# Packing two row groups for the last input transposes, and reading the parameter columns in one matmul, in a gated state-space and feed-forward kernel

## The chip, the cores and the metric

The kernel runs on one core of one Trainium2 chip. The metric is the device time of one execution in microseconds (us). The engines are named as in the profile: PE is TensorE (PEld its weight loads), DVE is VectorE, ACT is ScalarE, POOL is GpSimd, and SP is SyncE, which here only issues DMAs. ACT issues DMAs too; "SPq" and "ACTq" mark such issues. Row numbers such as L433 are lines of the kernel before the change.

## The reference

The input x has 2048 tokens of 448 values, in bf16. Three results are made of it and mixed token by token:

```python
g = sigmoid((x * gate_w).sum(-1, keepdims=True))
dt = exp(log_dt); Lam_bar = exp(dt * (Lambda_re + 1j * Lambda_im))
h[t] = Lam_bar * h[t-1] + B_bar @ x[t]          # complex scan over 2048 tokens, 448 states
a = 2 * real(C @ h[t]) + x * Dskip
b = silu(x @ w1) @ w2                           # 448 -> 1792 -> 448
out = g * a + (1 - g) * b
```

`B_bar` is B scaled by `(Lam_bar - 1) / Lam`. The three parameter vectors `log_dt`, `Lambda_re` and `Lambda_im` have 448 values each, one for each state.

## The kernel before

**Tiling.** The 2048 tokens are read as 1024 pairs: a row of `x2` is an even token followed by the odd one after it, 896 values. The feed-forward part works in four chunks of 512 tokens (even tokens first half and second half, then the odd ones). Its hidden width of 1792 is 14 blocks of 128 columns, taken two at a time. TensorE contracts over partitions, so x must be turned with features on partitions: three full groups of 128 features (j = 0, 1, 2) and a rest of 64 (j = 3, columns 384 to 447). A rest of 64 fills only half of the array's rows, so the kernel runs two matmuls side by side, one on partitions 0 to 63 ("LO") and one on 64 to 127 ("UP"). For that the rest of x has to lie on both halves: in `XT[0:64, 3, :]` and, copied, in `XR[64:128, :]`.

**The order of the work** is written out by hand. Each operation is given to an engine in program order, and a tracker (`Tracker`, L43 to L148) adds a semaphore wait for every read or written key that another engine or a DMA has touched. Each engine takes its list strictly in that order.

**The start.** Most of x is turned by DMA transposes, but the first chunk (tokens 0 to 511 of the even ones) is needed sooner. It is loaded as it lies, in four row groups k of 128 tokens (`XH[:, k, :]`, keys XA0 to XA3, and XB0 and XB1 for the later columns, which are the loads XA[4] and XA[5] in the code), and turned on TensorE by a matmul against the identity `ID`. `turn_k(j, k)` (L489) turns feature group j of row group k into PSUM; `turned_k` and `turned_x` (L499 to L508) are the DVE copies of the result into `XT`. Four such transposes per feature group are 16 in all, at L491. Between them TensorE begins the first six blocks of the hidden layer: `ffn1_first` (L427 to L441) is a generator that holds six PSUM banks open, contracts j = 0 over tokens 0 to 255 and then 256 to 511, and then j = 1 and j = 2 over all 512. Before anything has landed, `warm` (L477) runs 20 matmuls on ones, and two more ahead of the first real block (L515).

The rest (j = 3) is turned by four transposes at L535, each of 128 columns of which only the first 64 are used. `turned_x(3)` (L570) copies the 512 columns to `XT[:, 3, 0:512]`, and L571 copies the lower half of the same PSUM tile to `XR[64:128, 0:512]`. `ffn1_rem` (L443) then contracts the rest for two blocks at once, LO from `XT` and UP from `XR`, 512 columns each, three times for the six banks; after each, `ffn1_act` (L453) has ACT take Silu of two banks into `AT` (L455). From there on `pair` (L373) and `lanes` (L360, matmuls at L365) carry TensorE through the other blocks: a pair needs two free PSUM banks, and the first pair after the six banks that has to wait for one is the one that reuses the banks of `ffn1_act(0, 0)`.

**The parameters.** `log_dt`, `Lambda_re` and `Lambda_im` are loaded as three rows of `R` (`ld_row`, L261). DVE copies the last 64 values to a second place (`rd`, L465), four matmuls against four columns of `ID` turn the rows into four columns of 128 states each (`mm_cols`, L469), and one DVE copy brings them to `PV` (L528). ACT computes `dt` with Exp (L565), DVE makes the phase and `dt * Lambda_re` (L566 to L568), ACT makes `mag` with Exp (L569), and then loads the table with Silu by a small dummy activation (L572) before the first `ffn1_act`. A dummy Exp (L292) loads the Exp table early. The phase columns go on to POOL and DVE, which fill the rotation tables `FP`, `G` (L610 to L617).

**The queues.** Loads of x and of `w1` are issued on SP and ACT in turn (L275 to L301); ACT also issues the broadcasts of `gate_w` and `A_Dskip` (`GWB`, `DB`, L300 and L301), which DVE needs in `gate` and `skip` (L646 to L661). POOL makes `ID` and `IOTA` and clears a few columns (L324 to L332), and then waits for the phase columns.

Of the kernel before, what the change touches and what calls it, by code (L numbers as in the profile page):

```python
# [8 lines left out]
AF = mybir.ActivationFunctionType  # L9
# [141 lines left out]
def gated_mix(nc, A_x, A_Lambda_re, A_Lambda_im, A_B_re, A_B_im, A_C_re, A_C_im, A_log_dt,  # L151
              A_Dskip, B_x, B_w1, B_w2, gate_w, out):
    with ExitStack() as ctx:
# [3 lines left out]
        def sb(name, shape, dtype):  # L157
            return E(nc.sbuf_tensor(name, list(shape), dtype))
# [31 lines left out]
        R = sb("R", [128, 512], BF16)  # L190
        PV = sb("PV", [128, 4, 4], F32)
# [33 lines left out]
        def ld(eng, dst, src, key, group=None):  # L225
            return T.dma(eng, lambda e: e.dma_start(dst, src), writes=[key], group=group)  # L226
# [5 lines left out]
        XE = [(["XTe000", "XTe001", "XTe010", "XTe011", "XTe02"], ["XTe03"]), (["XTe1"], ["XTer1"])]  # L232
# [17 lines left out]
        def row(v):  # L250
            return v.rearrange("(o n) -> o n", o=1)
# [9 lines left out]
        def ld_row(eng, i, v):  # L261
            ld(eng, R[i:i + 1, 0:D], row(v), f"R{i}", gR if i < 2 else gR2)
# [23 lines left out]
        ld("sp", XH[:, 2:4, 384:512], x0[:, 2:4, 384:512], XA[5])  # L286
        gE = [ld_wr(eng, c, False) for c, eng in enumerate(("sp", "act"))]
# [4 lines left out]
        T.op("act", lambda e: e.activation(JK[:, 0:1], HP[:, :], AF.Exp), reads=["HP"], writes=["JK0"])  # L292
# [6 lines left out]

        ld_b(GWB, gate_w, "GW")  # L300
        ld_b(DB, A_Dskip, "DB")  # L301
# [29 lines left out]
        for pt in range(4):  # L331
            T.op("pool", lambda e, pt=pt: e.memset(HS[:, 2 * pt:2 * pt + 2, 0:8], 0.0), writes=[f"HSz{pt}"])  # L332
        SGN = ["SGa", "SGb"]
# [93 lines left out]
        def ffn1_first():  # L427
            banks = [nxt() for _ in range(NF1)]
            for j, h in ((0, 0), (0, 1), (1, None), (2, None)):
                c = slice(0, 512) if h is None else slice(256 * h, 256 * h + 256)  # L430
                for n, fb in enumerate((0, 2, 4, 1, 3, 5)):
                    bank = banks[fb]
                    T.op("pe", lambda pe, fb=fb, bank=bank, j=j, h=h, c=c: pe.matmul(  # L433
                        ps[:, bank, c], W1E[:, j, ff(fb) * 128:(ff(fb) + 1) * 128], XT[:, j, c],
                        start=(h == 0), stop=(h == 0), skip_group_check=(h != 0)),
                        reads=[f"W1Ej{j}" if j else f"W1Ej0{fb % 2}"] + (
                            ["XTe02"] if j == 2 else [f"XTe0{j}{h}"] if h is not None else [f"XTe0{j}0", f"XTe0{j}1"]),
                        writes=[f"ps{bank}"])
                    if (j, h, n) in ((0, 0, 3), (0, 0, 5), (1, None, 2), (1, None, 5)):
                        yield  # L440
            yield banks  # L441

        def ffn1_rem(banks, fb):  # L443
            def mm(pe):
                ins = None
                for i, p in enumerate((LO, UP)):
                    ins = pe.matmul(ps[:, banks[fb + i], :], w1(fb + i)(p, 3), xh(0, 0, 3, p), start=False, stop=True,  # L447
                                    skip_group_check=True)
                return ins
            T.op("pe", mm, reads=rem_ffn1(0, 0, fb), writes=[f"ps{banks[fb]}", f"ps{banks[fb + 1]}"])  # L450
            ffn1_act(0, fb, banks[fb], 2)
# [13 lines left out]
        def rd():  # L465
            T.op("dve", lambda e: e.tensor_copy(R[0:3, D:512], R[0:3, 384:448]), reads=["R0", "R1", "R2"],
                 writes=["Rd"])

        def mm_cols(pe):  # L469
            ins = None  # L470
            for pt in range(4):
                ins = pe.matmul(ps[:, 7, 256 + pt * 8:260 + pt * 8], R[:, pt * 128:(pt + 1) * 128],  # L472
                                ID[:, 0:4], start=True, stop=True)
            return ins
# [40 lines left out]
        warm(2, 4)  # L515
# [6 lines left out]
        for k in (2, 3):  # L522
# [5 lines left out]
        T.op("dve", lambda e: e.tensor_copy(  # L528
            PV[:, :, :], ps[:, 7, 256:288].rearrange("p (t c) -> p t c", c=8)[:, :, 0:4]),
            reads=["pv", "ps7"], writes=["PV"])  # L530
# [4 lines left out]
        for i in range(2):  # L535
            turn_x(3, i)
# [16 lines left out]
        LDT, LRE, LIM = PV[:, :, 0], PV[:, :, 1], PV[:, :, 2]  # L553
# [16 lines left out]
        turned_x(3)  # L570
        T.op("dve", lambda e: e.tensor_copy(XR[64:128, 0:512], xp[3][0:64, :]), reads=["ps7"], writes=["XR0a"])  # L571
        T.op("act", lambda e: e.activation(JK[:, 0:1], HP[:, :], AF.Silu), reads=["HP"], writes=["JK0"])  # L572
        pts("phr", col("phf"), MAGIC, -MAGIC, ALU.add, ALU.add, ["phf"])
# [688 lines left out]
```

## Time and profile before

| what | value |
|---|---|
| median of 3 runs | 136.72 us (136.67 to 136.77) |
| the profiled execution | 136.72 us, of which its span is 135.3 us |
| PE busy | 131.9 us, 97% of the span |
| DVE, ACT, POOL busy | 114.2, 93.7, 15.1 us |
| granted TensorE clock, all windows | 1.00 |
| DMA busy from 3 to 9 us | 0.96 to 0.98 of 16 engines |

The profile is of one execution. Times in it are microseconds from the start of the span; the 1.4 us between 135.3 and 136.72 lie outside the span. "Busy" counts instructions in flight, and TensorE's are pipelined, so the distance from one matmul's start to the next says more than its duration. A chain of waits leads from the last instruction back to what released it at each step; a timeline lists one engine's instructions in order, with start, duration, and in brackets the idle time before one and what ended it.

### The profile page before, as it was taken

How to read it: one execution, taken by the hardware profiler on the slowest of the kernel's cores; microseconds unless marked ns; L12 is line 12 of the kernel's file. 1: busy time of each engine (PE TensorE's matmuls, PEld its weight loads, DVE VectorE, ACT ScalarE, POOL GpSimd, SP SyncE). 2: the span in 40 equal slices, each digit the busy share in tenths (PEclk: the TensorE clock that was granted, in tenths of full speed). 3: DMA queues.
4: the chain of work that ended last, by engine and by line, in shares of the span. 5: the costliest groups of instructions: out<-in, count | busy, mean ns of one | idle time of the engine just before them, and what ended most of it. 6: DMA issues, size and time to landing. Idle time of an engine off the chain costs nothing.

```text
span 135.3 us, 2630 instructions
## 1 busy us (share of the span) xinstructions
PE 131.9 (97%) x1072; PEld 65.7 (49%) x1073; DVE 114.2 (84%) x152; ACT 93.7 (69%) x146; POOL 15.1 (11%) x32
## 2 busy tenths in 40 slices
PE   7899999999999999999999999999999999999993
PEld 7554444444444554444445544445555555555552
DVE  1467898917899798999999999999999999994554
ACT  0369888899939999768999597797113437879200
POOL 7108768050000000000000000000000000000000
DMA  4999979999897220000122000000000000222123
GB/s 109 273 278 162 157 153 244 181 286 300 251 184 123 55 62 0 0 0 0 44 56 60 5 0 0 0 5 0 0 0 0 0 0 7 100 89 81 68 78 126
DMA packets 24928, 11.95 MB, mean 88 GB/s; under 512 B 16851, under 2 KB 24406, under 8 KB 24918
## 3 DMA queue, kind: packets, MB, share of 16 engines
q1 hardware_dynamic: 22996, 10.43, 32.3%
q10 hardware_dynamic: 1922, 1.37, 3.6%
q8 instruction: 8, 0.13, 0.4%
q14 instruction: 2, 0.02, 0.0%
HBM read 5.51 MB, written 1.84 MB: 54 GB/s over the span
## 4 chain that ended last, share of the span: by engine, by line
PE 94%; DMA 3%; DVE 1%; ACTq 1%; issue 0%
PE ps L365 44%; PE ps L794 16%; PE ps L809 16%; PE ps L1047 15%; DMA XN<-in_A_x_dram 3%; PE ps L433 3%; DVE TMPS L1071 1%; ACTq L226 1%; PE ps L491 1%; PE ps L447 1%; PE ps L472 0%
## 5 line engine op out<-in xcount | busy, mean ns | idle before, releaser
L365 PE MATMUL ps<-XT,W1E 64*128 64x512 bf16 x325 | 41.3, 376 | 0.0
L455 ACT ACTIVATE AT<-ps 128x1024 bf16<-128x1024 f32 x28 | 28.2, 1019 | 7.4 <-PE ps L365 7.2
L365 PEld LDWEIGHTS ps<-XT,W1E 64*128 64x128 bf16 x325 | 16.9, 94 | 19.0 <-ACT AT L455 0.3
L365 PE MATMUL ps<-XT,BT 64*128 64x512 bf16 x156 | 22.4, 376 | 0.0
L809 PE MATMUL ps<-W,AT 64*128 64x448 bf16 x224 | 21.5, 349 | 0.0
L794 PE MATMUL ps<-W,AT 128*128 128x448 bf16 x112 | 21.4, 353 | 0.0
L794 PEld LDWEIGHTS ps<-W,AT 128*128 128x128 bf16 x112 | 10.9, 98 | 10.5 <-issue 0.4
L809 PEld LDWEIGHTS ps<-W,AT 64*128 64x128 bf16 x224 | 10.9, 94 | 10.4
L838 ACT ACTIVATE BT<-ps,GT 128x448 bf16<-128x448 f32 x8 | 5.1, 634 | 13.2 <-PE ps L794 13.2
L894 DVE SCALAR_TENSOR_TENSOR HS<-VE,P,ps 128x512 bf16<-128x512 bf16 (+1 forms) x13 | 9.6, 780 | 3.9 <-PE ps L365 3.9
L365 PEld LDWEIGHTS ps<-XT,BT 64*128 64x128 bf16 x156 | 8.1, 94 | 9.3 <-DVE HS L894 0.4
L938 DVE TENSOR_TENSOR_SCAN G<-P,Q 128x1024 f32<-128x1024 f32 (+1 forms) x6 | 11.4, 1923 | 0.0
L1047 PE MATMUL ps<-CO,VE 128*128 128x448 bf16 (+2 forms) x63 | 11.1, 332 | 0.0
L1047 PE MATMUL ps<-CO,HS 128*128 128x448 bf16 x56 | 11.1, 352 | 0.0
L365 PE MATMUL ps<-XR,W1E 64*128 64x512 bf16 x25 | 9.2, 376 | 0.0
L1047 PEld LDWEIGHTS ps<-CO,VE 128*128 128x128 bf16 x63 | 6.0, 98 | 4.8
L1047 PEld LDWEIGHTS ps<-CO,HS 128*128 128x128 bf16 x56 | 5.5, 98 | 5.1
L891 DVE TENSOR_TENSOR Q<-G,COS 128x2048 bf16<-128x2048 f32 (+1 forms) x4 | 7.0, 1755 | 0.1
L891 DVE TENSOR_TENSOR Q<-G,SIN 128x2048 bf16<-128x2048 f32 (+1 forms) x4 | 7.0, 1750 | 0.0
L856 ACT ACTIVATE VE<-ps 128x1024 bf16<-128x1024 f32 x6 | 6.1, 1020 | 1.2 <-PE ps L365 1.2
L858 ACT ACTIVATE ps<-VE,P 128x1024 f32<-128x1024 bf16 x6 | 6.7, 1118 | 0.2
L894 DVE SCALAR_TENSOR_TENSOR VE<-HS,P,FP 128x512 bf16<-128x512 bf16 (+1 forms) x7 | 6.6, 976 | 0.1
(123 smaller groups left out, 179.1 us busy)
## 6 DMA issues: line engine op xcount, KB each, us to landing
W<-in_B_w_dram SPq DMA_DIRECT2D x2, 784.0 KB, 6.6
XN<-in_A_x_dram SPq DMA_DIRECT2D x1, 896.0 KB, 5.1
out_dram<-OT SPq DMA_DIRECT2D x8, 112.0 KB, 1.7
out_dram<-TMPS SPq DMA_DIRECT2D x7, 112.0 KB, 1.7
HS<-HS SPq DMA_DIRECT2D x4, 128.0 KB, 2.3
XN<-in_A_x_dram SPq DMA_DIRECT2D x1, 384.0 KB, 3.7
W1E<-in_B_w_dram SPq DMA_DIRECT2D x1, 256.0 KB, 5.5
W1E<-in_B_w_dram ACTq DMA_DIRECT2D x1, 256.0 KB, 5.0
```

The source lines that it names most:

```text
L365: ins = pe.matmul(ps[:, bank, :], w(p, j), xh(odd, h, j, p), start=start and j == js[0], stop=stop and j == js[-1], skip_group_check=seeded)
L433: T.op("pe", lambda pe, fb=fb, bank=bank, j=j, h=h, c=c: pe.matmul(ps[:, bank, c], W1E[:, j, ff(fb) * 128:(ff(fb) + 1) * 128], XT[:, j, c] ...
L455: T.op("act", lambda e: e.activation(a[:, fb:fb + n, :], ps[:, bank:bank + n, :], AF.Silu), reads=[f"ps{bank + i}" for i in range(n)], wri ...
L794: ins = pe.matmul(ps[:, bank, 0:D], a[:, fb, q * 128:(q + 1) * 128], W2[:, ff(fb), :], start=(first and fb == 0), stop=(fb == NFB - 1), sk ...
L809: ins = pe.matmul(ps[:, bank, 0:D], a[p, fb, q * 128:(q + 1) * 128], W2[p, ff(fb), :], start=(start and fb == 0), stop=(not start and fb = ...
L838: T.op("act", lambda e: e.activation(bs(tile), ps[:, bank, 0:D], AF.Copy, scale=sc), reads=[f"ps{bank}", "GT2" if h else "GRI"], writes=ks)
L856: T.op("act", lambda e: e.activation(VE[:, m:m + 2, hs], ps[:, b[0]:b[0] + 2, :], AF.Copy), reads=[f"ps{i}" for i in b], writes=vs)
L858: T.op("act", lambda e: e.activation(ps[:, o[0]:o[0] + 2, :], VE[:, m:m + 2, hs], AF.Copy, scale=c1("lr", pt)), reads=vs + ["lr"], writes= ...
L891: T.op("dve", lambda e: e.tensor_tensor(o, a, b, op), reads=reads, writes=writes)
L894: T.op("dve", lambda e: e.scalar_tensor_tensor(o, a, s, b, ALU.mult, ALU.add), reads=reads, writes=writes)
L938: T.op("dve", lambda e: e.tensor_tensor_scan(G[:, c, w], rb, Q1[:, c, w], init, ALU.mult, ALU.add), reads=[f"Q1{c}", "rr", f"G{c}"], write ...
L1047: ins = pe.matmul(ps[:, bank, c], state(kt, odd, m), CO[:, m, c], start=False, stop=(m == YB[-1]), skip_group_check=True)
```

## The change

- **Last transposes.** POOL gets two copies after its clears (keys OT3 and X31). They put columns 384 to 447 of two row groups side by side into `OT[:, 3, 0:256]`: groups 0 and 2 into the first 128 columns, 1 and 3 into the next. Two transposes instead of four turn these, so that partitions 0 to 63 of the PSUM tile hold the rest of tokens 0 to 255, and 64 to 127 that of tokens 256 to 511. Three DVE copies of 256 columns take the place of the 512-column `turned_x(3)`: all partitions straight, upper half to lower, lower half to upper. `XT[0:64, 3]` then has the tokens in order, and `XT[64:128, 3]` the two halves exchanged.
- **The rest matmuls.** `ffn1_rem` reads both halves from `XT` and runs 256 columns at a time, LO and UP on opposite halves of the tokens: four matmuls for two blocks instead of two. The copy to `XR` stays, now from `XT` by `swap_xr`, after the three copies.
- **Parameter columns.** Each parameter vector is loaded as seven rows of 64 values (`R` shrinks from 512 columns to 128), `rd` doubles 21 rows, one matmul against 21 columns of `ID` turns them, and three DVE copies of 64 partitions instead of one of 128 fill `PV`, now indexed by vector first.
- **First blocks.** `ffn1_first` begins its blocks 0, 2 and 4 with 128 columns (row group 0 alone) and does columns 128 to 255 of these afterwards. One of the two late warm matmuls goes.
- **ACT's list.** The dummy Exp moves up in ACT's list, from ahead of its last `w1` issue to ahead of its last four, and the issues of `GWB` and `DB` move down, behind the dummy Silu.

```diff
-        R = sb("R", [128, 512], BF16)
-        PV = sb("PV", [128, 4, 4], F32)
+        R = sb("R", [128, 128], BF16)
+        PV = sb("PV", [128, 3, 4], F32)
...
-            ld(eng, R[i:i + 1, 0:D], row(v), f"R{i}", gR if i < 2 else gR2)
+            ld(eng, R[7 * i:7 * i + 7, 0:64], v.rearrange("(c n) -> c n", n=64), f"R{i}", gR if i < 2 else gR2)
...
         ld("sp", XH[:, 2:4, 384:512], x0[:, 2:4, 384:512], XA[5])
+        T.op("act", lambda e: e.activation(JK[:, 0:1], HP[:, :], AF.Exp), reads=["HP"], writes=["JK0"])
         gE = [ld_wr(eng, c, False) for c, eng in enumerate(("sp", "act"))]
...
-        T.op("act", lambda e: e.activation(JK[:, 0:1], HP[:, :], AF.Exp), reads=["HP"], writes=["JK0"])
...
-        ld_b(GWB, gate_w, "GW")
-        ld_b(DB, A_Dskip, "DB")
...
+        for i, key in enumerate(("OT3", "X31")):
+            T.op("pool", lambda e, i=i: e.tensor_copy(
+                OT[:, 3, 0:256].rearrange("p (k i c) -> p k i c", k=2, i=2)[:, :, i, :],
+                XH[:, 2 * i:2 * i + 2, 384:D]), reads=[XA[4 + i]], writes=[key])
...
+            for fb in (0, 2, 4):
+                T.op("pe", lambda pe, fb=fb, bank=banks[fb]: pe.matmul(
+                    ps[:, bank, 0:128], W1E[:, 0, ff(fb) * 128:(ff(fb) + 1) * 128], XT[:, 0, 0:128],
+                    start=True, stop=True), reads=["W1Ej00", "XTe000a"], writes=[f"ps{banks[fb]}"])
...
-                c = slice(0, 512) if h is None else slice(256 * h, 256 * h + 256)
+                    k = h == 0 and n < 3
+                    c = slice(0, 512) if h is None else slice(128 if k else 256 * h, 256 * h + 256)
...
-                for i, p in enumerate((LO, UP)):
-                    ins = pe.matmul(ps[:, banks[fb + i], :], w1(fb + i)(p, 3), xh(0, 0, 3, p), start=False, stop=True,
-                                    skip_group_check=True)
+                for o in (0, 256):
+                    for i, p in enumerate((LO, UP)):
+                        w = (o + 256 * i) % 512
+                        ins = pe.matmul(ps[:, banks[fb + i], w:w + 256], w1(fb + i)(p, 3), XT[p, 3, o:o + 256],
+                                        start=False, stop=True, skip_group_check=True)
...
-            T.op("dve", lambda e: e.tensor_copy(R[0:3, D:512], R[0:3, 384:448]), reads=["R0", "R1", "R2"],
+            T.op("dve", lambda e: e.tensor_copy(R[0:21, 64:128], R[0:21, 0:64]), reads=["R0", "R1", "R2"],
...
-            for pt in range(4):
-                ins = pe.matmul(ps[:, 7, 256 + pt * 8:260 + pt * 8], R[:, pt * 128:(pt + 1) * 128],
-                                ID[:, 0:4], start=True, stop=True)
+            return pe.matmul(ps[:, 7, 256:277], R[:, :], ID[:, 0:21], start=True, stop=True)
...
-        warm(2, 4)
+        warm(1, 4)
...
-        T.op("dve", lambda e: e.tensor_copy(
-            PV[:, :, :], ps[:, 7, 256:288].rearrange("p (t c) -> p t c", c=8)[:, :, 0:4]),
-            reads=["pv", "ps7"], writes=["PV"])
+        PX = ps[:, 7, 256:277].rearrange("p (i c) -> p i c", c=7)
+        for p, t, c, key in ((LO, slice(0, 4), slice(0, 7, 2), "PVa"), (UP, slice(0, 3), slice(1, 6, 2), "PVb"),
+                             (UP, slice(3, 4), slice(6, 7), "PV")):
+            T.op("dve", lambda e, p=p, t=t, c=c: e.tensor_copy(PV[p, 0:3, t], PX[p, :, c]),
+                 reads=["pv", "ps7"], writes=[key])
...
         for i in range(2):
-            turn_x(3, i)
+            T.op("pe", lambda pe, i=i: pe.transpose(
+                xp[3][:, i * 128:(i + 1) * 128], OT[:, 3, 128 * i:128 * i + 128], ID[:, :]),
+                reads=["OT3", "X31", "ID"], writes=[f"ps{PB[3]}"])
...
-        turned_x(3)
-        T.op("dve", lambda e: e.tensor_copy(XR[64:128, 0:512], xp[3][0:64, :]), reads=["ps7"], writes=["XR0a"])
+        for p, q, o, key in ((slice(0, 128), slice(0, 128), 0, "a"), (LO, UP, 256, "b"), (UP, LO, 256, "c")):
+            T.op("dve", lambda e, p=p, q=q, o=o: e.tensor_copy(XT[p, 3, o:o + 256], xp[3][q, 0:256]),
+                 reads=["ps7"], writes=["XTe03" + key])
+        swap_xr("dve", 0, 0)
         T.op("act", lambda e: e.activation(JK[:, 0:1], HP[:, :], AF.Silu), reads=["HP"], writes=["JK0"])
+        ld_b(GWB, gate_w, "GW")
+        ld_b(DB, A_Dskip, "DB")
```

More of the change, by code (lines that the diff above doesn't have):

```diff
@@ L230, in ldt @@
                          writes=[key, *also], group=group)
-        XE = [(["XTe000", "XTe001", "XTe010", "XTe011", "XTe02"], ["XTe03"]), (["XTe1"], ["XTer1"])]
+        XE = [(["XTe000", "XTe001", "XTe010", "XTe011", "XTe02"], ["XTe03a", "XTe03b", "XTe03c"]), (["XTe1"], ["XTer1"])]
         XO = [([f"XTo{h}"], [f"XTr{h}"]) for h in range(2)]
@@ L428, in ffn1_first @@
             banks = [nxt() for _ in range(NF1)]
+            for fb in (0, 2, 4):
+                T.op("pe", lambda pe, fb=fb, bank=banks[fb]: pe.matmul(
+                    ps[:, bank, 0:128], W1E[:, 0, ff(fb) * 128:(ff(fb) + 1) * 128], XT[:, 0, 0:128],
+                    start=True, stop=True), reads=["W1Ej00", "XTe000a"], writes=[f"ps{banks[fb]}"])
             for j, h in ((0, 0), (0, 1), (1, None), (2, None)):
-                c = slice(0, 512) if h is None else slice(256 * h, 256 * h + 256)
                 for n, fb in enumerate((0, 2, 4, 1, 3, 5)):
+                    k = h == 0 and n < 3
+                    c = slice(0, 512) if h is None else slice(128 if k else 256 * h, 256 * h + 256)
                     bank = banks[fb]
-                    T.op("pe", lambda pe, fb=fb, bank=bank, j=j, h=h, c=c: pe.matmul(
+                    T.op("pe", lambda pe, fb=fb, bank=bank, j=j, h=h, c=c, k=k: pe.matmul(
                         ps[:, bank, c], W1E[:, j, ff(fb) * 128:(ff(fb) + 1) * 128], XT[:, j, c],
-                        start=(h == 0), stop=(h == 0), skip_group_check=(h != 0)),
+                        start=(h == 0 and not k), stop=(h == 0 and not k), skip_group_check=(h != 0 or k)),
                         reads=[f"W1Ej{j}" if j else f"W1Ej0{fb % 2}"] + (
@@ L445, in mm @@
                 ins = None
-                for i, p in enumerate((LO, UP)):
-                    ins = pe.matmul(ps[:, banks[fb + i], :], w1(fb + i)(p, 3), xh(0, 0, 3, p), start=False, stop=True,
-                                    skip_group_check=True)
+                for o in (0, 256):
[3 more added lines that the diff above has]
+                                        start=False, stop=True, skip_group_check=True)
                 return ins
-            T.op("pe", mm, reads=rem_ffn1(0, 0, fb), writes=[f"ps{banks[fb]}", f"ps{banks[fb + 1]}"])
+            T.op("pe", mm, reads=["W1Er0", "W1Er1", *XE[0][1]], writes=[f"ps{banks[fb]}", f"ps{banks[fb + 1]}"])
             ffn1_act(0, fb, banks[fb], 2)
@@ L465, in rd @@
         def rd():
-            T.op("dve", lambda e: e.tensor_copy(R[0:3, D:512], R[0:3, 384:448]), reads=["R0", "R1", "R2"],
+            T.op("dve", lambda e: e.tensor_copy(R[0:21, 64:128], R[0:21, 0:64]), reads=["R0", "R1", "R2"],
                  writes=["Rd"])
         def mm_cols(pe):
-            ins = None
-            for pt in range(4):
-                ins = pe.matmul(ps[:, 7, 256 + pt * 8:260 + pt * 8], R[:, pt * 128:(pt + 1) * 128],
-                                ID[:, 0:4], start=True, stop=True)
-            return ins
+            return pe.matmul(ps[:, 7, 256:277], R[:, :], ID[:, 0:21], start=True, stop=True)
         ones = nc.const_aps.tensor(1.0, [128, 128], BF16)
@@ L551, in c1 @@
             return P[:, i, pt:pt + 1]
-        LDT, LRE, LIM = PV[:, :, 0], PV[:, :, 1], PV[:, :, 2]
+        LDT, LRE, LIM = PV[:, 0, :], PV[:, 1, :], PV[:, 2, :]
         def pts(o, a, s1, s2, op0, op1, ra):
```

## The prediction

> **What bounds the kernel now.** I read the chain of waits first, in order of time, then the timelines of DVE and ACT over the first 17 us, then the waits of PE's weight loads.
>
> ```profile
> 1.71 3.59 DMA XN<-in_A_x_dram
> ...
> 5.34 0.23 PE ps L491
> ...
> 7.37 0.08 PE ps L472 x4
> 7.45 0.24 PE ps L491 x4
> 7.75 0.59 PE ps L433 x2
> 8.34 0.22 PE ps L491 x4
> 8.56 1.29 PE ps L433 x6
> 9.86 0.76 PE ps L447 x6
> 10.61 31.76 PE ps L365 x294
> ```
>
> A load of x (row group 3) lands at 1.71 + 3.59 = 5.30 us and releases a transpose at 5.34. From there TensorE is the chain without a break until 132.76 us. What PE saves before 5.34 only lengthens its wait there (the waits put 0.6 us of PEld's idle time to that load). What it saves after 5.34 shortens the run, unless something else takes its place. The change touches PE only up to about 10.5 us, so two more lists matter.
>
> ```profile
> 7.49 0.17 DVE L528 COPY PV<-ps 128x16 f32<-128x16 f32 x1 [1.04 <-PE ps L472]
> 7.73 0.42 DVE L507 COPY XT<-ps 128x512 bf16<-128x512 bf16 x1
> 8.07 0.15 DVE L566 SCALAR_TENSOR_TENSOR P<-PV,P 128x4 f32<-128x4 f32 x1
> 8.14 0.16 DVE L559 TENSOR_TENSOR P<-P,PV 128x4 f32<-128x4 f32 x1
> 8.60 0.42 DVE L507 COPY XT<-ps 128x512 bf16<-128x512 bf16 x1 [0.30 <-PE ps L491]
> 9.06 0.42 DVE L571 COPY XR<-ps 64x512 bf16<-64x512 bf16 x1
> ```
>
> ```profile
> 5.61 1.28 ACT L292 ACT_TABLE_LOAD   x1 [5.61 <-DVE XT L501]
> 5.68 0.55 ACTq L226 DMA_DIRECT2D W1E<-in_B_w_dram  x1
> ...
> 8.56 1.28 ACT L572 ACT_TABLE_LOAD   x1
> 9.85 0.20 ACT L572 ACTIVATE JK<-HP 128x1 bf16<-128x1 f32 x1
> 10.22 1.94 ACT L455 ACTIVATE AT<-ps 128x1024 bf16<-128x1024 f32 x2 [0.17 <-PE ps L447]
> ```
>
> DVE copies `PV` and then x group 2 (7.73 to 8.15), and PE reads that copy at 8.40, so the copy is 0.25 us early. ACT waits 0.17 us for the first rest matmuls, so the Silu table is that early. Behind it there is no room: the first Silu ends at 11.25, and PE's weight load at L365 waits for it until 11.30, just when its matmul is due.
>
> **The change, part by part** (on the profiled execution, 136.72 us: span 135.3 and 1.4 outside; it equals the median).
>
> *PE work removed.* In PE's timeline the four column matmuls run from 7.21 to 7.31, 0.025 each; one instead of four saves 0.075. The four last transposes run from 8.18 to 8.40, 0.055 each; two less save 0.11. Sum: 0.185 us off the path, if nothing else is late.
>
> *PE work added.* The split first blocks are three more matmuls of 128 columns, all before 4.68, with 0.23 us of idle before and 0.6 after the transpose there: nothing. Were that cover gone, three weight loads of 0.1 each, at most 0.3. The rest matmuls have the same columns in twice the pieces: two of 256 columns are 0.11 apart (5.41 to 5.63), one of 512 takes 0.215, so six pieces add about 0.01.
>
> *POOL's packing.* The loads it needs land at 2.19 + 3.9 = 6.1 and 3.28 + 4.0 = 7.3 (sizes of 128 and 64 KB in the table of DMAs). POOL has been idle since 4.2. No row shows such a copy; between the clear of 128 columns (0.20) and the cast of 1024 (1.04) I take 0.25, nearest in size, so the second copy is done at 7.6, while PE wants it at about 8.1. At 1.04 it ends at 8.4 and costs 0.3.
>
> *Three copies for PV, and what they push back.* This is the disputed term. The column matmul still starts at 7.21, and being one, its result is ready 0.07 sooner: DVE starts at 7.42 instead of 7.49. How soon DVE takes the next copy varies in the trace: L566 and L559 overlap by 0.08 (8.07 + 0.15 against 8.14), but L571, which moves data to the other half of the partitions, starts 0.03 after its predecessor's end though it waits for nothing, and so does the operation after it. The second `PV` copy goes from the lower half to the upper: 7.42 + 0.17 + 0.03 = 7.62. The third stays in the upper: overlapping, 7.62 + 0.09 = 7.71, end 7.88. The copy of x group 2 goes back to all partitions: start 7.91, end 7.91 + 0.42 = 8.33, where it was 8.15. From the end of a copy to PE's start the trace shows 0.05 (L501 to 5.89) to 0.12 (3.65 to 3.77, where two things are waited for, as here). I take 0.12: PE goes on at 8.45. It is ready at 8.40 - 0.185 = 8.215, so it waits 0.23, and the saving has become a loss of 0.05. Bounds: with every copy overlapping, x group 2 ends at 8.09 and PE keeps its 0.185; with none, 7.42, 7.62, 7.82, 8.02, end 8.44, PE at 8.56, a loss of 0.16.
>
> The page "VectorE: DVE Perf Modes" of the Trainium skill speaks against this part: in "Rules for kernel authors" it says of chained operations that the pipeline empties after each regardless, and to keep their number small. The rows above differ for operations on the same partitions (0.08 of overlap); by the page's rule the sum would be the upper bound, 0.16 lost.
>
> *Behind it.* Six matmuls of group 2 take 1.29 and the change from 128 to 64 rows about 0.1 (9.70 to 9.79; the same 0.1 stands at 90.69, L365 to L794, with no wait), so the rest matmuls start at 9.85 against 9.79. DVE must have the three copies of the rest by then: the transposes are done at 8.41; the copies take 0.29 each for 256 columns (as L507 at 5.94), the second and third with 0.03 before them, so 9.34. Covered by 0.5; and `XR`, copied from SBUF in 0.29 (L241) by 9.66, is first read at 10.89. ACT: `PV` at 7.88, `dt` until 8.12, phase and product at 8.25 behind the x copy, `mag` at 8.51, table from 8.73 to 10.01, dummy Silu until 10.23, where ACT was ready at 10.06. The first Silu is wanted 0.43 after the rest matmuls start, at 10.28: just covered, and PE's 11.30 moves with it.
>
> *The rest.* POOL's and DVE's rotation tables start 0.2 later; DVE then waits 3.9 us in all for PE at L894, so that is absorbed. The earlier dummy Exp changes nothing, since `PV` comes last. `GWB` and `DB` are issued at about 8.6 and 9.1 instead of 6.26 and 6.78, take 5 to 6 us to land, and are first used after 23 us. Their issues now stand between the dummy Silu and the first real one in ACT's list: 0.49 + 0.45. At 5.61 and 5.68 the trace shows ACT issuing a DMA while a table load runs, ahead of the dummy behind it, so the table load of 1.28 hides them.
>
> *Sum.* 0.05 of later start, 0.01 for the pieces: **136.72 + 0.06 = 136.78 us**, and by the bounds of the copies 136.54 to 136.89.
>
> **The rivals.**
>
> *All copies overlap (chance 0.18).* Then the removed work is the gain: 136.72 - 0.185 + 0.01 = 136.54. For it: most neighbouring DVE operations overlap by 0.08. Against it: every copy in the trace that changes halves starts 0.03 after its predecessor's end.
>
> *The load at 5.30 comes sooner (0.12).* The same 96 KB took 2.9 us on SP's queue and 3.6 on ACT's. The parameter rows, now 21 short pieces instead of 3, are issued while it is under way, so its order among other packets may shift. If it took 2.9, PE could go on at 4.7, 0.6 sooner; I take half, as other loads follow closely: 136.78 - 0.3 = 136.5, at best 136.2. Nothing ahead of it in its queue changes, which speaks against it. I count this case as faster by over 0.2%, at 136.4.
>
> *The parameter rows land late (0.14), the case that ends on the other side.* `rd` began at 6.27, so the rows were in by then; as 128-byte pieces over more partitions they can land as late as the load issued behind them on SP, 7.28. `rd` needs 0.17 and PE 0.05, so from 6.95 on PE waits at the column matmul, and everything behind shifts. At 7.28 the matmul starts at 7.54 instead of 7.21: 136.78 + 0.33 = 137.1.
>
> *ACT's DMA issues are not hidden (0.05).* If they waited for the dummy Silu at 10.2, the first Silu would start at 11.2 instead of 10.28, and PE's wait at 11.30 would grow by 0.9: 137.7. The row at 5.68 speaks against it.
>
> *The clock (0.05).* Matmuls of 128 columns stand 0.105 apart at first (20 from 0.82 to 2.92) and 0.055 later; the step comes near 4.2, 3.4 us after the first. One warm matmul less could miss it; were it to come another 3.4 us later, at 7.6, PE's 2.3 us from 5.34 on would go at half rate: 1.1 lost, 137.9. The same 0.1 us is idle twice over before 4.7 already, so I give it little. "TensorE: Matmul & The Clock Gate" of the Trainium skill, in "The HAM clock gate", says that a window of 3.4 us decides, which starts by itself and counts activity, not instructions; by that rule one matmul less in a busy window changes nothing in most runs, and a missed window would cost half of 3.4, or 1.7, an estimate from that page.
>
> That the change does not do what it says is in the forecast already: the halved transposes are real, and only their gain is spent.
>
> **How the numbers follow.** Forecast 0.46, all copies overlapping 0.18, load sooner 0.12, rows late 0.14, ACT 0.05, clock 0.05. A measurement of this kernel can tell about 0.2%, 0.27 us, from no change. Forecast and overlap lie within it: same 0.64. Load sooner: faster 0.12. The other three: slower 0.24. The range takes in the forecast, the overlap and the late rows, 136.52 to 137.11, and leaves 0.22 out.
>
> **What would show it.** In the changed profile: the copy of x group 2 starts near 7.9 and ends near 8.33, and the first L433 matmul behind the last transposes waits for it until about 8.45; a gap of 0.03 before the second `PV` copy and before the x copy, an overlap before the third. The column matmul at 7.21 shows the rows in time. POOL's copies end by 7.7. ACT's first Silu starts near 10.28. The last load of x in the chain ends near 5.3. I am wrong if PE enters the rest matmuls before 9.65 or after 10.0, or if a transpose starts away from 5.34.

## The result, and the profile after

The changed kernel takes 138.80 us (median of four runs, 137.68 to 139.49), the kernel before 136.75 on the same chip: a ratio of 1.0139, 95% interval 1.0105 to 1.0172. A second measurement on another chip gave 138.65 (138.04 to 139.71) against 136.49, 1.0159 (1.0124 to 1.0193). Medians, ranges and ratios, here and below, leave out slow runs: those at a lower granted clock (here 141.11 and 141.37, at 0.988) and those over 1.5% above their kernel's fastest, of which e5 and e6 below have two each, at 138.4 to 138.9 with the clock at 1.00, so that a loss of the kernel's own may be left out with them. The forecast was 136.78, a loss of 0.06 and too small to measure, in a range that ended at 137.11; the loss is about 2 us, and the runs spread far more than those of before.

The profiled execution took 138.40 us: a span of 136.8 (1.5 more than before) and 1.6 outside it (1.4 before). Its chain of waits (start, duration, what) no longer runs through TensorE from 5.3 us on:

```profile
3.86 4.37 DMA W1E<-in_B_w_dram
8.23 0.02 issue
8.24 0.02 SPq L146
8.26 0.05 issue
8.31 8.94 DMA XT<-in_A_x_dram
17.25 0.05 issue
17.29 26.54 PE ps L366 x244
```

The long step is SP's first DMA transpose of x (the even tokens of pairs 512 to 1023). It takes 8.94 us to land. In the second measurement's profile it takes 8.50 (8.43 to 16.93). Before, the same one was issued at 8.60 and landed at 14.15, after 5.55. SP's timeline of before, and the line of its DMA table from 8 to 18 us (the last number is the median time from issue to landing of both transposes of x, in us; it is 8.1 after):

```profile
8.60 3.94 SPq L229 DMA_TRANSPOSE XT<-in_A_x_dram  x2
```

```profile
XT<-in_A_x_dram SPq DMA_TRANSPOSE x2, 5.8
```

PE's timeline of the changed kernel shows both losses of the span:

```profile
7.43 0.17 PE L478 MATMUL ps<-ID,R 128*128 128x21 bf16 x1
7.46 0.38 PE L495 MATMUL ps<-ID,XN 128*128 128x128 bf16 x4
7.89 0.59 PE L439 MATMUL ps<-XT,W1E 128*128 128x512 bf16 x2
8.32 0.28 PE L542 MATMUL ps<-ID,OT 128*128 128x128 bf16 x2
8.71 1.46 PE L439 MATMUL ps<-XT,W1E 128*128 128x512 bf16 x6
10.10 0.83 PE L455 MATMUL ps<-XT,W1E 64*128 64x256 bf16 x12
10.76 1.02 PE L366 MATMUL ps<-XT,W1E 64*128 64x512 bf16 x7
...
15.95 0.38 PE L366 MATMUL ps<-XR,W1E 64*128 64x512 bf16 x1
17.29 0.39 PE L366 MATMUL ps<-XT,W1E 64*128 64x512 bf16 x2 [0.97 <-DMA XT<-in_A_x_dram]
```

Matmuls of 512 columns stand 0.21 apart, so the one at 17.29 was due at 16.16: **1.13 us of waiting for the transposes** (the row's 0.97 counts from the end of the matmul before). The first pair at L366 starts at 10.76 (10.45 before): 0.31 in the front. From 17.29 on the two kernels run alike (116.93 us to the end of TensorE's part of the chain; 116.91 before, from the same matmul at 15.85). The front, on DVE and on ACT:

```profile
7.66 0.44 DVE L535 COPY PV<-ps 64x12 f32<-64x12 f32 x3 [1.35 <-PE ps L495]
8.14 0.42 DVE L511 COPY XT<-ps 128x512 bf16<-128x512 bf16 x1
...
8.64 0.93 DVE L579 COPY XT<-ps 128x256 bf16<-128x256 bf16 x3
9.60 0.29 DVE L241 COPY XR<-XT 64x512 bf16<-64x512 bf16 x1
```

```profile
8.75 0.34 ACTq L226 DMA_DIRECT2D GWB<-in_gate_w_dram  x1
8.96 1.28 ACT L582 ACT_TABLE_LOAD   x1
9.12 0.57 ACTq L226 DMA_DIRECT2D DB<-in_A_Dskip_dram  x1
10.25 0.20 ACT L582 ACTIVATE JK<-HP 128x1 bf16<-128x1 f32 x1
10.53 1.94 ACT L463 ACTIVATE AT<-ps 128x1024 bf16<-128x1024 f32 x2
```

The three `PV` copies and the x copy behind them follow each other as forecast, all 0.2 later: the x copy ends at 8.56 and block 2 starts at 8.71, 0.33 after the second of the last transposes at 8.38. The two issues are hidden by the table load, as forecast. What they move is not. The next lines are the rates of the DMA engines from 8 to 18 us, GB/s in slices of 0.25 us, before and after:

```profile
GB/s 310 311 320 340 302 267 231 152 96 79 82 114 163 209 104 40 103 95 266 290 292 281 285 240 56 134 139 189 21 9 10 131 292 286 262 161 181 243 289 293
```

```profile
GB/s 316 322 311 313 303 266 130 173 162 175 48 58 31 20 21 0 9 219 112 119 254 252 126 31 274 339 313 269 208 0 0 5 9 9 131 294 229 287 294 274
```

Before, the broadcasts have ended (their last packet starts at 12.27) when the transposes get their run at 240 to 292 GB/s (12.5 to 14.0 us), and XT lands right behind it, at 14.15. After, both kinds of packets are in flight from 10.1 us on, and almost nothing moves from 10.5 to 12.25 (0 to 58): the 28 packets of 896 bytes that the broadcasts start there take 0.58 us each on average and up to 1.8, where they took 0.07 before (9 to 12.5 us). The transposes' run starts at 13.0 only, is broken by a dip to 31 GB/s before 14.0, and goes on until 15.25. A second hole follows in each kernel, 15.0 to 15.75 before and 15.25 to 16.5 after. XT was in ahead of it before, and not after.

The second profile of the changed kernel (`e13_changed_again`) tells the two holes apart:

```profile
GB/s 269 324 330 354 327 281 228 147 95 101 75 65 118 132 58 81 87 174 42 64 103 64 82 131 282 289 287 278 326 17 4 0 8 9 10 240 283 242 291 290
```

Here the engines never stop before 15 us; they move 42 to 174 GB/s from 10 to 14.0, with the packets of both kinds mixed. The run starts at 14.0, the hole of 15.25 to 16.75 catches its end, and PE waits 1.22 us. So the loss does not need the near stop; what both profiles share is that the run is late enough to meet the second hole.

### The profile page after: what moved, and what is told of

The parts are those of the page before. It is cut to its first block, busy times and chain, and to the rows that moved or that the text cites. A ratio compares the mean times of both kernels' runs of the same rounds, so it can differ in the third digit from the quotient of the medians.

```text
span 136.8 us, 2645 instructions
## 1 busy us (share of the span) xinstructions
PE 132.8 (97%) x1075; PEld 66.3 (49%) x1076; DVE 114.6 (84%) x156; ACT 93.7 (69%) x146; POOL 16.0 (12%) x34
## 4 chain that ended last, share of the span: by engine, by line
PE 85%; DMA 10%; ACTq 2%; DVE 1%; issue 0%; ACT 0%; SPq 0%
PE ps L366 39%; PE ps L806 16%; PE ps L821 15%; PE ps L1059 15%; DMA XT<-in_A_x_dram 7%; DMA W1E<-in_B_w_dram 3%; ACTq L226 2%; DVE TMPS L1083 1%; ACT L287 0%; SPq L146 0%
## 5 line engine op out<-in xcount | busy, mean ns | idle before, releaser
L366 PE MATMUL ps<-XT,W1E 64*128 64x512 bf16 x325 | 41.5, 376 | 1.0 <-DMA XT<-in_A_x_dram 1.0
L366 PEld LDWEIGHTS ps<-XT,W1E 64*128 64x128 bf16 x325 | 16.8, 94 | 20.1 <-DMA XT<-in_A_x_dram 1.5
L366 PE MATMUL ps<-XT,BT 64*128 64x512 bf16 x156 | 22.4, 376 | 0.0
L806 PEld LDWEIGHTS ps<-W,AT 128*128 128x128 bf16 x112 | 10.9, 98 | 10.5 <-issue 0.4
L366 PEld LDWEIGHTS ps<-XT,BT 64*128 64x128 bf16 x156 | 8.1, 94 | 9.4 <-DVE HS L906 0.4
L366 PE MATMUL ps<-XR,W1E 64*128 64x512 bf16 x25 | 9.2, 376 | 0.0
```

The costliest lines, as they stand in the source:

```text
L366: ins = pe.matmul(ps[:, bank, :], w(p, j), xh(odd, h, j, p), start=start and j == js[0], stop=stop and j == js[-1], skip_group_check=seeded)
L806: ins = pe.matmul(ps[:, bank, 0:D], a[:, fb, q * 128:(q + 1) * 128], W2[:, ff(fb), :], start=(first and fb == 0), stop=(fb == NFB - 1), sk ...
```

## The experiments

**Theories.** T1: the moved issues of `GWB` and `DB` make their packets meet the transposes. T2: one warm matmul less lets the clock step up later. T3: the 21 short parameter rows, or another part, delay the transposes. Each group of runs shared one chip (the fourth group two) and the runs of the kernel before (136.5 to 136.7 throughout). "Outside" is the mean over all runs of a kernel of its time less its span; before: 1.40.

### First group: the issues and the warm matmul

`e1_rows_back`, the changed kernel with the two issues at their old place, ahead of `load_xn`:

```diff
-        ld_b(GWB, gate_w, "GW")
-        ld_b(DB, A_Dskip, "DB")
...
+        ld_b(GWB, gate_w, "GW")
+        ld_b(DB, A_Dskip, "DB")
```

> The changed kernel with one part undone: GWB and DB are issued where they were before the change, ahead of the moved-down place. Theory 1 (the moved issues make the broadcast packets meet SP's transposes, which land late and stop PE): the first transposes land near 14.2 us again, the 1.0 us wait of PE on XT near 16 to 17 us is gone, and the median falls from 139.3 to 137.0 (136.72 plus the 0.3 that the front of the change costs), with a spread under 0.5. Rival (21 short parameter rows, or the earlier Exp, delay the transposes): the wait stays, 139 with the same spread.

Measured: 137.06 (136.91 to 137.35), ratio 1.0034 (1.0022 to 1.0047). The long wait and the spread are gone, as T1 has it. But XT landed at 15.94, not 14.2, only just in time. The rates of this kernel from 8 to 18 us show why:

```profile
GB/s 334 363 340 330 310 299 285 242 216 162 85 132 122 60 134 116 57 48 95 131 282 294 290 335 267 132 16 0 7 9 10 210 289 232 292 293 269 291 292 292
```

The transposes' run starts at 13.0 instead of 12.5, and the second hole (14.5 to 15.75) catches its end. ACT issued the two broadcasts at 6.71 and 7.23 here, 6.26 and 6.78 before.

`e2_rows_late`, the kernel before with the two lines moved down, as in the change.

> The kernel before with one part of the change alone: GWB and DB are issued behind the dummy Silu. Theory 1: the transposes issued near 8.6 land near 17 instead of 14.2, PE waits about 1 us for XT near 16, and the median rises to 138 to 139, with a spread of 1 us or more. Rival (the delay needs the other parts of the change): 136.7, no wait.

Measured: 136.60, eleven of twelve runs at 136.42 to 136.99 and one at 138.11; 1.0011 (0.9991 to 1.0032). XT landed at 14.86 in the profile. With e1, moving the issues is needed for the full loss, and alone it seldom makes one.

`e3_rows_back_warm2`, e1's kernel with this, and `e4_one_warm`, the kernel before with the reverse of it:

```diff
-        warm(1, 4)
+        warm(2, 4)
```

> The first experiment's kernel with the second late warm matmul back as well. Theory 2 (the clock steps up at 6.8 instead of 4.2 because one matmul of warming is missing): the step is back near 4.2, the first blocks run at 0.11 us for 256 columns, and the time is 0.2 to 0.3 below that of the first experiment. Rival (the step is set by the time at which the window falls, not by one matmul): the step stays near 6.8 and the two times agree within 0.1.

> The kernel before with one late warm matmul instead of two and nothing else changed. Theory 2: the clock steps up near 6.8 instead of 4.2 and the time rises by 0.2 to 0.3, to about 137.0. Rival (the split first blocks, or the phase of the window, move the step): the step stays near 4.2 and the time at 136.72.

Measured: 137.12 (136.72 to 137.66), 1.0036 (1.0020 to 1.0051), and 136.63 (136.18 to 137.10), 0.9997 (0.9983 to 1.0012). **T2 falls**: the warm matmul does nothing in either. The pitch of matmuls stepped up by 4.2 us with one warm matmul (e4), and near 6.8 in `e2_rows_late`, which has two, as before.

### Second group: the parts one by one

`e5_act_list_back`, e1's kernel with the dummy Exp back as well; `e6_act_list_only`, the kernel before with both changes of ACT's list (the reverse of this diff, and the two issues moved down):

```diff
-        T.op("act", lambda e: e.activation(JK[:, 0:1], HP[:, :], AF.Exp), reads=["HP"], writes=["JK0"])
         gE = [ld_wr(eng, c, False) for c, eng in enumerate(("sp", "act"))]
...
+        T.op("act", lambda e: e.activation(JK[:, 0:1], HP[:, :], AF.Exp), reads=["HP"], writes=["JK0"])
         ld_w3("sp", 0, 1, FB, F_FF, "e")
```

> The changed kernel with both changes of ACT's list undone: GWB and DB at their old place and the dummy Exp again ahead of the last w1 issue. In the first experiment (only GWB and DB back) ACT issued the two at 6.70 and 7.22 us instead of 6.26 and 6.78, the first transposes landed at 15.94 instead of 14.15, and PE wants them at about 15.65 to 15.95. Theory 1a (the Exp ahead of ACT's issues is what makes these 0.45 later, and this makes the transposes late): they land near 14.2, no PE wait on XT, time 136.7 to 136.85. Rival 1b (the 21 short parameter rows delay the loads): landing near 15.9 as in the first experiment, 137.0 to 137.1.

Measured: 136.94 (136.56 to 137.19, one run at 138.55), 1.0036 (1.0009 to 1.0062). XT landed at 14.34 in the profile, with the 21 rows in place, so these do not by themselves delay it. That it was the Exp's place which made it 15.94 in e1 fits, but e8 below has 15.64 with the Exp unmoved. The time did not come back with XT, so something else costs 0.4; and what the run at 138.55 waited for was not profiled.

> The kernel before with both changes of ACT's list and nothing else. Moving GWB and DB alone gave 136.6 with the first transposes at 14.86. Theory 1a (the list as a whole makes the collision): transposes near 17, PE waits 1 us, 138 to 139. Rival 1b (the 21 short rows are needed for it): transposes near 14.9 and 136.6 to 136.8.

Measured: two levels among the ten runs counted, six at 136.26 to 136.93 and four at 137.38 to 137.83; 1.0024 (0.9995 to 1.0053). The profiled run is of the lower level, with XT at 15.04. I read the upper level as runs with XT late, as T1 has it, but none of them was profiled; neither theory expected both levels in one kernel.

`e7_columns_only` (the hunks on `R`, `PV`, `rd`, `mm_cols`) and `e8_transposes_only` (those on POOL's copies, `ffn1_rem`, the two transposes and the three copies), each on the kernel before.

> The kernel before with the parameter columns alone changed: 21 rows of 64, one matmul, three copies to PV. By the prediction's step: the column matmul saves 0.075, the three copies end the x copy 0.18 later, PE goes on at about 8.45 instead of 8.40: 136.75. Theory 1b (21 rows delay the loads and with them the transposes): landing near 15.9 and 137.0 or more. If all is hidden: 136.65.

> The kernel before with the halved transposes alone: POOL's two copies, two transposes, three copies of 256 columns, rest matmuls in halves. By the prediction: 0.11 saved on PE and 0.01 added, 136.55 to 136.6. Rival (POOL's second copy waits for the last load of x, which landed at 7.19 to 8.03 in the runs so far, and takes 0.3, so PE waits for it where that load is late): 136.7 to 136.9.

Measured: 136.81 (136.60 to 137.28), 1.0009 (0.9986 to 1.0032), XT at 13.99; and 136.81 (136.46 to 137.07), 0.9999 (0.9975 to 1.0024), XT at 15.64. The prices are read from PE's timelines, columns first:

```profile
7.19 0.17 PE L470 MATMUL ps<-ID,R 128*128 128x21 bf16 x1
...
10.52 0.81 PE L365 MATMUL ps<-XT,W1E 64*128 64x512 bf16 x6
```

```profile
7.30 0.24 PE L478 MATMUL ps<-ID,R 128*128 128x4 bf16 x4
...
8.28 0.27 PE L542 MATMUL ps<-ID,OT 128*128 128x128 bf16 x2
...
10.45 0.81 PE L369 MATMUL ps<-XT,W1E 64*128 64x512 bf16 x6
```

From the column matmul to the first pair is 3.24 us in all profiles with neither part, 3.30 to 3.33 with the columns, 3.15 with the halved transposes and 3.31 to 3.34 with both (3.51 once, where the last load of x held up POOL's copy until PE wanted it). So the halved transposes earn 0.09 of PE's time alone, and nothing beside the three `PV` copies; in the time of the whole kernel e8 does not show the 0.09 (0.9999, with 0.3 us either way). When the column matmul starts (6.67 to 7.60) goes with no part of the change, but with the step of the clock: 7.40 on average in the seven profiles where the pitch stepped up after 6 us, 7.02 in the others.

### Third group: the collision and the time outside

`e9_rows_behind_x`, the changed kernel, and `e12_halved_rows_behind_x`, e8's kernel, with the broadcasts on SP behind the transposes of x:

```diff
-            ld("act", dst[:, :], row(src).partition_broadcast(128).rearrange("p o n -> p (o n)"), key)
+            ld("sp", dst[:, :], row(src).partition_broadcast(128).rearrange("p o n -> p (o n)"), key)
...
         ldt(XT[:, 3:4, 512:1024], x2[512:1024, 384:512], "XTer1")
+        ld_b(GWB, gate_w, "GW")
+        ld_b(DB, A_Dskip, "DB")
```

> The changed kernel with GWB and DB issued on SP, behind the two transposes of x and ahead of those of B, so that their packets follow those of XT in the same queue. Theory 1 (the broadcast packets hold up XT's): XT lands by 14 us, ahead of the stretch of about 1.3 us around an instruction fetch in which the DMA engines move next to nothing, PE does not wait for XT in any run, and the time is that of the kernel before plus the 0.08 us of the front and the 0.19 us that the changed kernels spend outside the span: 136.85 to 136.95, spread under 0.8. Rival (another part of the change makes XT late): above 137.5.

Measured: 137.17 (136.94 to 137.32), 1.0043 (1.0028 to 1.0059). XT landed at 14.74, PE waited for it nowhere in the profile, the spread is 0.4: the late XT is gone. But 1.76 us lie outside the span, 0.17 more than in the changed kernel.

> An attempt at a better version: the kernel before with the halved transposes alone, and with GWB and DB issued on SP behind the transposes of x. Column matmul to first pair was 3.15 us in the halved kernel and 3.25 before: 0.10 saved, 0.055 lost outside the span, and no run in which XT is late: 136.5 to 136.55 where the kernel before is at 136.6. If DVE needs GWB or the transposes of B sooner than they land, 136.7 or more.

Measured: 136.91 (136.63 to 137.50), 1.0032 (1.0017 to 1.0048): slower than before. PE's 0.09 is there (3.15), and 1.67 outside (1.45 in e8) takes more away.

`e10_split_only`, the hunk on `ffn1_first` on the kernel before.

> The kernel before with the split first blocks alone (three more matmuls). The time outside the span was 1.40 us in the kernel before, 1.455 with the columns alone, 1.455 with the halved transposes alone, and 1.59 in all kernels with the whole change. If that time adds up part by part, the split brings the missing 0.08: outside 1.48, the span unchanged, 136.65 to 136.7. If not, outside 1.40 and 136.55 to 136.6.

Measured: 136.54 (136.36 to 136.99), 0.9996 (0.9981 to 1.0011), outside 1.39. Split blocks cost nothing, inside or outside.

`e11_other_rows`, the changed kernel with:

```diff
-        ld_b(GWB, gate_w, "GW")
-        ld_b(DB, A_Dskip, "DB")
+        ld("act", GWB[:, :], B_w1[0:128, 0:448], "GW")
+        ld("act", DB[:, :], B_w1[128:256, 0:448], "DB")
```

> The changed kernel, in which GWB and DB are filled at the same place and in the same size, not with one row of 896 bytes read 128 times, but with 128 different rows of w1 (so that gate and skip are computed with wrong factors). If the reading of one row by all engines is what stops the queues near 11 us, these loads land in 3 us or less, XT lands by 14.5, and the time is 136.9 to 137.1. If any 224 KB there do it, 138 to 139.5 as in the changed kernel.

Measured: 137.12 (136.84 to 138.12), 1.0055 (1.0031 to 1.0079). Neither number: six of nine runs at 136.84 to 137.15, three from 137.6 up. In the profile, one of those three, `GWB` landed at 12.53, 4.25 us after its issue (5.4 and 5.3 in the changed kernel's two profiles), and XT still only at 16.53. With one row read 128 times the loss is larger (1.0139 and 1.0159 there), but other bytes in as many packets of the same size can make XT late too.

### Fourth group: what makes it sure, and what lies outside

`e13_changed_again` is the changed kernel as it is; `e14_list_and_columns` is e6 with e7's hunks, `e15_list_and_halved` e6 with e8's.

> The changed kernel itself, on the chip of the three runs beside it, as their control. If the collision is in the program: 138 to 139.5 again, XT later than 16.5 us, PE waiting for it in the profile. If the chip of the first runs made it: about 137.0 in most runs.

> The kernel before with ACT's list and the parameter columns changed, without the halved transposes and the split. If the 21 short rows make the collision sure: 138 to 139.5. If not: as with the list alone, 136.3 to 137.8, median about 137, plus 0.2 for the columns.

> The kernel before with ACT's list and the halved transposes changed, without the columns and the split. If the three copies of the rest or POOL's copies are needed for the collision: 138 to 139.5. If not: as with the list alone, median about 137.

Measured: 138.65 (138.04 to 139.71); 137.05 (136.59 to 137.74), 1.0044 (1.0024 to 1.0065); 137.45 (136.95 to 138.45), 1.0077 (1.0045 to 1.0108). The loss is in the program, not in a chip. The ratios rise from the list alone (1.0024) over these two to the whole change (1.0159), though only the last is clear of its neighbour's interval. No single part makes it sure, so T3 does not hold in its simple form; the moved issues are the one part without which it was rare.

`e16_four_dve`, the kernel before with:

```diff
+        for i in range(4):
+            T.op("dve", lambda e, i=i: e.memset(SG[64:128, 1:2], 1.0), writes=["SGx"])
```

> The kernel before with four more small DVE instructions at the start (clears of a column that nothing reads), as many as the change adds to DVE. If the time outside the span goes with DVE's number of instructions: outside 1.55 to 1.6 instead of 1.40, the span unchanged, 136.8. If not: 1.40 and 136.6.

Measured: 136.73 (136.49 to 137.14), 1.0018 (1.0005 to 1.0031); outside 1.62, the span as before. Four clears that nothing waits for put 0.22 us on the time, none of it within the span. The first line of this kernel's page and that of the kernel before:

```profile
PE 132.0 (98%) x1073; PEld 65.5 (48%) x1073; DVE 114.5 (85%) x156; ACT 93.8 (69%) x146; POOL 14.4 (11%) x32
```

```profile
PE 131.9 (97%) x1072; PEld 65.7 (49%) x1073; DVE 114.2 (84%) x152; ACT 93.7 (69%) x146; POOL 15.1 (11%) x32
```

`e18_three_fewer_dve`, the kernel before with this, and `SGa` and `SGb` in the same way:

```diff
-        T.op("dve", lambda e: e.memset(HP[:, :], HALF_PI), writes=["HP"])
+        T.op("pool", lambda e: e.memset(HP[:, :], HALF_PI), writes=["HP"])
```

> The kernel before with three small clears moved from DVE to POOL. Four more DVE instructions put 0.22 us on the time outside the span. If three fewer take some away again: outside 1.25 to 1.35 instead of 1.40, the span unchanged, 136.45 to 136.55 where the kernel before is at 136.6: a version faster than both. If 1.40 is a floor: 136.6.

Measured: 136.48 (136.32 to 136.92), 0.9992 (0.9974 to 1.0011), outside 1.41. By DVE's instructions on the page: 149 and 152 give 1.39 to 1.41 outside; 154 gives 1.45 to 1.48; 156 gives 1.59 to 1.63, in seven kernels (e9 and e12, with the broadcasts on SP, lie above). It is not linear, 1.40 is its floor here, and why it is so stays open.

`e17_rows_behind_silu`, the changed kernel with the two issues moved past two of the first Silus:

```diff
         ffn1_rem(first, 2)
+        ld_b(GWB, gate_w, "GW")
+        ld_b(DB, A_Dskip, "DB")
         pact("sn", col("fr"), AF.Sin, ["fr"], scale=SIN_SCALE)
```

> The changed kernel with GWB and DB issued on ACT two Silus later, at about 12.5 us, when both transposes of x have been issued (8.3 to 12.3). Theory 1: XT lands by 14 us, PE does not wait for it, and what stays is 0.08 us in the front and 0.2 us outside the span: 136.8 to 136.95. Rival (the place on ACT's queue matters, not the collision with XT): 137.7 or more.

Measured: 136.94 (136.33 to 137.02) against 136.56; the ratio 1.0011 (0.9992 to 1.0031). The issues ran at 10.50 and 10.88, sooner than I had thought, and still behind enough:

```profile
GB/s 311 320 295 342 293 225 126 161 216 159 194 289 293 287 180 132 173 79 32 64 23 104 125 184 122 57 122 126 133 153 76 75 127 281 292 278 287 216 275 290
```

The transposes have a run (287 to 293) from 10.75 on, before the broadcasts' first packet at 11.96; XT landed at 13.76, PE never waited for it, and the chain of waits is TensorE's again from 0.83 us, but for the `PV` and x copies of DVE from 7.41 to 8.45. This shows T1 most directly: same work, same queues, the two issues 1.75 us later than in the first profile of the changed kernel, and the loss falls from 2.2 us (138.65 against 136.49, e13) to 0.4. The second hole is missing here, but XT was in before the time at which it begins elsewhere. None of the versions is measurably faster than the kernel before.

## Why the prediction was wrong

**The step that failed** is the sentence on `GWB` and `DB`: issued at 8.6 and 9.1, "take 5 to 6 us to land, and are first used after 23 us". Both halves held, nearly (8.75 and 9.12; 5.4 and 7.8 us), and the cost of nothing drawn from them did not. It asked who waits for the two loads. It did not ask which transfers they share the 16 engines with: SP's transposes were issued at the same moment, and PE took their result at 15.85 before, 1.7 us after it landed: that was all the margin there was, and the landing moved by 3.1 us (14.15 to 17.25). It counted ACT's own queue with care and left out SP's. Undone in three ways (e1, e9, e17), the loss of 2.2 us falls to between 0.4 and 0.55.

What remains has two parts. **A term was missing**: the 1.4 us outside the span were taken as fixed, and four more DVE instructions make them 1.6. **The front** was right in mechanism and nearly in size: forecast +0.06 from the column matmul to the first pair, measured +0.09. Together they are about 0.3 of the 0.4 to 0.55.

Point by point:

- *Three copies of PV.* Forecast 7.42, 7.62, 7.71, x copy from 7.91 to 8.33, block 2 at 8.45, 1.24 after the column matmul. Measured 7.66, 7.86, 7.95, 8.14 to 8.56, 8.71, and 1.28. The two changes of halves cost 0.03 each and the third copy overlapped, as the rows had said. The upper bound, which is also the sum by the page "VectorE: DVE Perf Modes" of the Trainium skill ("Rules for kernel authors"), was not reached: by it block 2 would have come 1.35 after the column matmul. (By the forecast's own steps of 0.09 the lower bound ends the x copy at 8.11, not 8.09, which changes nothing.)
- *Halved transposes.* 0.095 forecast net, 0.09 measured alone on PE (e8), all of it lost beside the columns.
- *POOL's packing.* 0.25 forecast, 0.29 measured; done at 7.92. It cost 0.2 once (e1), where its load landed at 8.03.
- *Split blocks, dummy Exp, ACT's issues.* The first free (e10). The issues are hidden. The Exp ahead of ACT's `w1` issues goes with issues behind it that come 0.45 later (6.71 against 6.26).
- *Rivals.* The load of x did come sooner (4.71 instead of 5.30) in this one profile, and PE gained nothing, since its clock stepped up only near 6.8: 256 columns took 0.213 until then and 0.11 after. The granted clock reads 1.00 in these windows, so the pitch is the evidence. PE entered the rest matmuls at 10.10, past the 10.0 that the forecast gave as a sign of being wrong, because the column matmul began 0.22 late. Over 20 profiles load and step vary by themselves. The rows were in time. The clock's step is not set by one matmul; "TensorE: Matmul & The Clock Gate" of the Trainium skill, section "The HAM clock gate", has its window start by itself, and e3 and e4 agree. The price of 1.1 us was for a step at 7.6, which no profile shows; a step after 6 us went with a column matmul 0.4 later.

"DMA: Bandwidth & Descriptors" of the Trainium skill, section "Queues, rings and completion order", says that an engine takes packets from its queues in turn. That one queue's packets then delay another's agrees with the later landing; the size (8.94 and 8.50 us instead of 5.55) only the runs show, and that the engines nearly stop does not follow from it. The same page's "Rules for kernel authors" says that a transpose next to ordinary DMAs needs nothing; that is meant of correctness, and for time the runs here say otherwise (8.94 us with the broadcasts beside it, 5.5 in e17 ahead of them).

**What stays open.** Why the whole change loses 1 us or more in every run and ACT's list alone in four of ten. Over the profiles, XT was latest (16.5 to 17.5 us) where `GWB` was issued within 0.45 us of the first transpose, and landed at 14.9 to 15.75 where the two lay 0.6 to 0.9 apart, to either side. Larger distances mostly helped: 2.2 us later XT landed at 13.76 (e17), 3.0 and 3.6 us later at 14.4 and 14.75 (e12, e9), and 1.2 us and more earlier at 14.0 to 14.4 in seven profiles. But it landed at 15.6 to 15.95, just in time, in three others (e1, e3, e8) with 1.7 to 1.8 us, so distance is not all. What these three share with the late ones is that the second hole began (at 14.25 to 16.0) before XT was in. Two issues of 0.3 to 0.5 us that fall into the same stretch would mix their packets most, but that is argued and not shown. The second hole came, in all profiles but e17's, 0.2 to 1.3 us after the start of a 16 KB packet of the instruction queue (13.85 us before, 14.75 after); that one causes the other was not tried.

## What to carry to other kernels

A DMA that is moved has two costs: when its own reader needs it, and which transfers in flight it now meets; list what every queue has under way at the new moment, and the margin of each of those transfers to its reader. A broadcast of one row to 128 partitions is 128 packets of 896 bytes here, and two of them made a transpose of x land 3 us later, so keep them away from DMA transposes that an engine is about to need. Look at the spread as well as the median: where runs suddenly vary by more than 1%, as here, look for a transfer close to its deadline.

## What was not expected of the hardware

- The time outside the span depends on the program: 1.40 us with up to 152 DVE instructions, 1.45 to 1.48 with 154, 1.59 to 1.63 with 156, and 0.17 to 0.21 more with two DMA issues moved from ACT's queue to SP's (e9, e12).
- Broadcasts and transposes in flight together can bring the engines almost to a stop: 0 to 58 GB/s for 1.75 us, with 175 before it and 219 after, in one profile of the changed kernel; the other shows 42 to 174 there.
- A hole of 0.5 to 1.5 us, in which the DMA engines move 0 to 28 GB/s, follows the start of a fetch of 16 KB of instructions in all profiles but one. Where it began after 14 us, a first transpose of x that was in ahead of it landed at 13.99 to 15.75, and one that was not at 15.64 to 17.5.
- The step of the TensorE clock, read from the pitch of matmuls, came anywhere from before 3.9 us (e1, e3, e13) to between 6.5 and 6.8 (after, e2), in the same kernel too (after, e13).
